# Remaking the instruction order of a planned attention and Fourier-mixing kernel from a table of measured landing times

## The chip, the cores and the metric

The kernel runs on one core of one Trainium2 chip, in a single launch. The metric is the device time in microseconds, the median of several runs. The core has five engines with an instruction stream each: TensorE (PE, matmuls), VectorE (DVE), ScalarE (ACT), GpSimd (POOL) and SyncE (SP, which here only issues transfers). Transfers between device memory and on-chip memory are carried by 16 DMA engines.

## The reference

Batch 4, 8 heads, 768 positions, 64 elements for each head. First comes an attention with a local window of 96 positions and 8 global ones, and a distance bias for each head:

```python
scores = scale * np.matmul(q, k.transpose(0, 1, 3, 2))
is_global = pos[None, :] < 8
is_local = (rel >= 0) & (rel < 96)          # rel = query position - key position
dist = np.where(is_global & ~is_local, 96.0, np.abs(rel))
scores = np.where(is_global | is_local, scores - slopes * dist, -1e9)
a = softmax(scores)
x = heads_side_by_side(a @ v)               # (4, 768, 512)
```

Then a block that mixes with a two-dimensional Fourier transform, normalises, and runs a two-layer MLP:

```python
u = x + np.real(np.fft.fft(np.fft.fft(x, axis=1), axis=2))
un = (u - mean(u)) / np.sqrt(var(u) + 1e-6)
out = u + np.maximum(un @ w_ch1, 0.0) @ w_ch2     # 512 -> 2048 -> 512
```

## The kernel before

The order of all instructions is made by a small planner in Python when the kernel is built. Each piece of work is announced with what it needs, which engine could do it, and how long that takes by a formula. The planner keeps a clock for each engine (`t`) and the time at which each result is there (`tok`); it takes whichever piece could start first, emits its instructions, and moves the clock. Nothing of these clocks is in the program that runs: there the engines wait for each other by semaphores, and each engine takes its instructions in the order in which the planner emitted them.

```python
class Plan:
    SEM = 0.06
    LAND = {("xw", 0, 0): 33.0, ("xw", 0, 1): 37.0, ("xr", 0): 43.0}
    LAT = {"ACT": 0.14, "DVE": 0.12, "POOL": 0.08}
    ...
    def emit(self, place):
        ...
        end = self.t[eng] = ends[i]
        if dma:
            q = "DMA2" if eng == "ACT" or outs and outs[0][0] in ("xw", "xr") else "DMA"
            end = self.t[q] = max(self.t[q], end) + dma
        else:
            lat += self.LAT.get(eng, 0.0)
        for o in outs:
            self.tok[o] = max(end + lat, self.LAND.get(o, 0.0)) if dma else (end + lat, eng)
        ...
    def run(self, streams):
        # [cut] of the heads of the PE streams, and of the work waiting for other
        # engines, take what can start first; emit it; go on until all is done
```

`LAND` holds times before which a transfer's result is not taken as there. `("xw", 0, n)` is the attention output of batch 0 on its way out to device memory, in two parts, and `("xr", 0)` its way back in another row order.

There are four streams of PE work, by order of precedence: `MIX` (Fourier blocks, normalisation), `ATT` (attention), `PH` (first MLP layer) and `PG` (second). The first two may be taken out of order within the next ten pieces.

**Attention, batches 0 and 1.** q, k and v come in for each pair of heads (`hp` 0 to 3; `n` is 4 times the batch plus `hp`). q and k are cast and turned by PE (`trans`, in traces "pt", copied to `qkT`); scores are built in three blocks for a pair ("sc", lines 553, 558 and 563), and ScalarE takes the exp ("ex"). v is cast by GpSimd (line 420, "er"), turned by PE ("pvp") and copied out half by VectorE and half by ScalarE (lines 454 and 455):

```python
def cast_v0(b, hp):
    ...
    pl.later([("POOL", 0.87, cast)], [("ld", n, 2)] + free("er", n), 0.0, [("vc", n)], ...)

def v_place(b, hp):
    ...                                        # 12 matmuls into pvp, then two copies into v16
    ATT.append(([("vc", n), ("c", "id")], BANKS(b), run))
```

`("ld", n, 2)` is the landing of v of pair n. "pgl" and "eg" are the scores of the global positions, "pav" the product with v, lines 709 and 710 its division by the sum, which gives x.

**Loads.** SyncE issues q, k, v; GpSimd issues the weights, eight transfers of 512 KB, which are cast on the way:

```python
pl.later([("SP", 0.55, run)], free(*vat(n)) + [("xi",)] * (n >= HP), 0.0, [("ld", n, 2)], lat=1.7, dma=1.45)
...
pl.later([("POOL", 0.85, lambda i=i: wload(i))], needs, 0.0,
         [("w1" if i < 4 else "w2", i % 4)], lat=2.2, dma=2.75, rank=0, ...)
...
pl.later([("SP", 0.45, hold)], [("w2", 3)], 0.0, [("gate",)])    # batches 2 and 3 load after the last weights
```

**Fourier blocks.** VectorE folds x (lines 754 to 865), PE transforms along the positions ("py", line 891, copied by lines 906 and 908), GpSimd mirrors (lines 926 to 939), PE transforms along the features ("pu", line 971), and VectorE adds x back (lines 990 and 999), which gives u. ScalarE scales the row sum (line 1011), ScalarE or VectorE makes the centred row un (lines 1021 and 1023), and PE turns it ("ptu"), copied to unT (lines 1070 and 1072). ScalarE squares un for the variance (line 1030), and GpSimd turns that into the scale (lines 1037 and 1038).

**MLP.** Rows come in twelve blocks c of 256. For the first layer eight "ph" units of 8 matmuls (128x256) need unT of the block and a quarter of w1; ScalarE or VectorE takes the relu into hT (lines 1096 and 1097). For the second layer "pg" units of 4 matmuls (128x512) need hT and a quarter of w2; VectorE adds u (line 1122), and the rows leave. The last four blocks use a form with fewer multiplications ("pgA", "pgD").

```python
def ph_unit(c, jp):
    needs = [("unT", c), ("w1", jp // 2)] + (free("hT", 5 + c) if jp == 0 else []) + [("CD",)]
    ...
def pg_unit(c, t, part):
    needs = [("h", c, 2 * part), ("h", c, 2 * part + 1), ("w2", part)]
```

PSUM, where PE writes, is divided into two tiles "xx" of two banks each, and two early tiles "C" and "D" of two banks each, which serve batch 0 and parts of batch 1 and are then given up for the accumulators of ph and pg; `("CD",)` is that handover.

Of the kernel before, what the change touches and what calls it, by code (L numbers as in the profile page):

```python
# [17 lines left out]
class Plan:  # L18
# [5 lines left out]


    SEM = 0.06
    LAND = {("xw", 0, 0): 33.0, ("xw", 0, 1): 37.0, ("xr", 0): 43.0}
    LAT = {"ACT": 0.14, "DVE": 0.12, "POOL": 0.08}

    def __init__(self):  # L30
# [56 lines left out]
    def emit(self, place):  # L87
# [11 lines left out]
        for o in outs:  # L99
            self.tok[o] = max(end + lat, self.LAND.get(o, 0.0)) if dma else (end + lat, eng)  # L100
        for u in uses:
# [1373 lines left out]
```

## Time and profile before

| | |
|---|---|
| device time, median of 3 runs | 273.59 us (272.04 to 274.04) |
| profiled span, mean granted PE clock | 272.5 us, 0.987 |
| PE busy | 257.0 us, 94% of the span, 2540 matmuls |
| VectorE busy | 172.0 us, 63% |
| ScalarE busy | 153.4 us, 56% |
| GpSimd busy | 58.3 us, 21% |
| HBM read and written | 31.92 MB and 9.44 MB |

How to read it: the ends of matmuls are modelled, so PE can be "busy" without being at its peak; the distance from one matmul's start to the next says more. A stretch without matmuls is a real hole. In the chain of work that ended last, PE has 73% of the span, DMA 11% and VectorE 8%. Of PE's time ph has 95.4 us and pg 60.2 us. The eight weight transfers take 19.7 us from issue to landing in the median, the three v loads of batch 1 that go to "qs" 16.8 us.

### The profile page before, as it was taken

Reading aid. Unit: us, or ns where it says so; the run is one execution under the profiler, and the core shown is the slowest. Engines: PE = TensorE matmul, PEld = TensorE weight load, DVE = VectorE, ACT = ScalarE, POOL = GpSimd, SP = SyncE. Lnnn points to the kernel's source line nnn. Section 1 sums busy time; section 2 is a strip of 40 time slices with the busy share of each in tenths; the row PEclk is TensorE's granted clock in tenths of the full one; section 3 lists DMA queues with packets and bytes.
Section 4 is the critical chain, followed back from the end, with each engine's and each line's share of the span. In section 5 each row is a group of like instructions: output and inputs, shape, how many; then the busy total and the mean of one; then the engine's idle time right before and its main releaser. Section 6 shows DMA issues by size and latency. Waiting matters only on the chain.

```text
span 272.5 us, 6257 instructions
## 1 busy us (share of the span) xinstructions
PE 257.0 (94%) x2540; PEld 182.6 (67%) x2540; DVE 172.0 (63%) x349; ACT 153.4 (56%) x267; POOL 58.3 (21%) x123
## 2 busy tenths in 40 slices
PE   7898899679999899999999999899999999999994
PEld 3444668347876776667567457576877668888883
DVE  4547855721789665445348976786999765445273
ACT  1579785746639737987683046799435245453310
POOL 1433298133120052311231004021100402010000
PEclk9999999959999999999999999999999999999999
DMA  7999969999569976969776995431036151412022
GB/s 210 290 290 285 330 159 243 214 216 211 140 112 248 260 178 131 182 161 148 176 179 159 188 284 147 75 89 39 2 81 192 38 114 44 98 20 79 0 81 77
DMA packets 75743, 42.03 MB, mean 154 GB/s; under 512 B 32834, under 2 KB 71746, under 8 KB 75714
## 3 DMA queue, kind: packets, MB, share of 16 engines
q1 hardware_dynamic: 68658, 32.71, 51.1%
q0 software_dynamic: 4224, 4.19, 9.3%
q10 hardware_dynamic: 2832, 4.72, 6.8%
q8 instruction: 20, 0.33, 0.5%
q14 instruction: 9, 0.07, 0.1%
HBM read 31.92 MB, written 9.44 MB: 152 GB/s over the span
## 4 chain that ended last, share of the span: by engine, by line
PE 73%; DMA 11%; DVE 8%; SPq 4%; POOL 1%; issue 1%; ACT 1%; DVEq 0%; POOLq 0%; ACTq 0%
PE ph L1090 29%; PE pg L1113 18%; DMA qs<-in_v_dram 6%; PE pgD L1194 5%; PE pgA L1194 4%; PE pav L690 3%; PE sc L563 3%; SPq L371 3%; DMA qs<-in_q_dram 3%; PE pu L971 3%; PE py L891 2%; DMA xd<-x 2%; PE pav L679 1%; PE ptu L1062 1%; SPq L1273 1%
## 5 line engine op out<-in xcount | busy, mean ns | idle before, releaser
L1090 PE MATMUL ph<-unT,w 128*128 128x256 f16 x768 | 95.4, 275 | 0.8 <-DVE hT L1097 0.8
L1090 PEld LDWEIGHTS <-w 128*128 128x128 f16 x768 | 73.1, 99 | 15.6 <-issue 4.8
L1096 ACT ACTIVATE hT<-ph 128x512 f16<-128x512 f32 x75 | 44.6, 596 | 47.5 <-PE ph L1090 47.4
L1113 PE MATMUL pg<-w,hT 128*128 128x512 f16 x256 | 60.2, 379 | 0.0
L1113 PEld LDWEIGHTS <-hT 128*128 128x128 f16 x256 | 24.3, 98 | 24.3 <-issue 0.8
L586 ACT ACTIVATE ex<-sc 128x992 f16<-128x992 f32 (+2 forms) x24 | 21.0, 928 | 8.3 <-PE sc L563 8.3
L583 ACT ACTIVATE er<-sc 128x992 f16<-128x992 f32 (+2 forms) x24 | 21.8, 923 | 3.6 <-PE sc L563 3.5
L598 DVE TENSOR_TENSOR ex<-er,mk 128x992 f16<-128x992 f16 (+2 forms) x24 | 14.8, 626 | 12.0 <-ACT er L583 11.9
L375 ACT ACTIVATE qk<-qs 128x384 f16<-128x384 f32 (+1 forms) x33 | 15.4, 522 | 12.1 <-DMA qkT<-qk 8.3
L939 POOL COPY ww<-zy 128x512 f16<-128x512 f16 x16 | 9.2, 609 | 53.2 <-PE py L891 52.2
L1097 DVE TENSOR_SCALAR hT<-ph 128x512 f16<-128x512 f32 x21 | 14.5, 688 | 8.4 <-PE ph L1090 8.1
L563 PE MATMUL sc<-qkT 64*128 64x256 f16 (+1 forms) x192 | 17.5, 264 | 1.4 <-ACT unT L1070 0.8
L1122 DVE SCALAR_TENSOR_TENSOR u<-pg,sm,u 128x512 f32<-128x512 f32 x16 | 12.0, 747 | 8.8 <-PE pg L1113 8.8
L690 PE MATMUL pav<-v,ex 128*128 128x65 f16 x352 | 16.4, 193 | 0.8 <-DVE x L710 0.7
L563 PEld LDWEIGHTS <-qkT 64*128 64x128 f16 x192 | 5.8, 94 | 16.4 <-issue 14.4
L690 PEld LDWEIGHTS <-ex 128*128 128x128 f16 x352 | 15.3, 97 | 2.1 <-DVE x L710 0.9
L1030 ACT ACTIVATE un<-un 128x512 f16<-128x512 f16 x24 | 14.9, 621 | 1.1 <-DMA unT<-un 1.0
L465 POOL CAST v<-qs 128x768 f16<-128x768 f32 x8 | 7.7, 965 | 35.3 <-DMA qs<-in_v_dram 35.3
L1021 ACT ACTIVATE un<-u,sm 128x512 f16<-128x512 f32 x13 | 9.2, 719 | 10.4 <-DVE sm L994 10.3
L906 ACT ACTIVATE zy<-py 128x1024 f16<-128x1024 f32 (+1 forms) x11 | 9.0, 827 | 10.7 <-PE py L891 10.2
L990 DVE SCALAR_TENSOR_TENSOR u<-pu,xr 128x512 f32<-128x512 f32 x18 | 11.7, 687 | 4.3 <-PE pu L971 4.3
L1194 PEld LDWEIGHTS <-hT 128*128 128x128 f16 x128 | 12.5, 98 | 2.1 <-issue 0.4
(129 smaller groups left out, 373.8 us busy)
## 6 DMA issues: line engine op xcount, KB each, us to landing
out_dram<-u SPq DMA_DIRECT2D x24, 256.0 KB, 2.2
w<-in_moe_w_ch_dram POOLq DMA_DIRECT2D x8, 512.0 KB, 19.7
qs<-in_q_dram SPq DMA_DIRECT2D x9, 384.0 KB, 4.5
qs<-in_k_dram SPq DMA_DIRECT2D x9, 384.0 KB, 5.8
qs<-in_v_dram SPq DMA_DIRECT2D x16, 192.0 KB, 4.2
xr<-xd ACTq DMA_DIRECT2D x3, 768.0 KB, 4.8
u<-in_v_dram SPq DMA_DIRECT2D x5, 384.0 KB, 7.2
w<-in_q_dram SPq DMA_DIRECT2D x4, 384.0 KB, 6.4
```

The source lines that it names most:

```text
L375: A(d, s, AF.Copy)
L563: nc.tensor.matmul(pa[:, s, c0:c0 + cw], TT[n][lo:lo + 64, 1, i * P:(i + 1) * P], TT[n][lo:lo + 64, 0, i * P:i * P + cw], start=(b > 1), s ...
L583: A(mine(), cut(pa), AF.Exp, 0.0, 0.125)
L586: A(cut(expst[hp][:, :, g * 512:g * 512 + (384 if g == 2 else 512)]), cut(pa), AF.Exp, 0.0, 0.125)
L598: VT(o, mine(), m, op=ALU.mult)
L690: nc.tensor.matmul(po[:, jj, hh * 65:(hh + 1) * 65], lhsT, v16[b % 2][:, i, h, 0:65], start=(jp == 0 and a == 0), stop=(a == len(ops) - 1) ...
L1030: A(x, x, AF.Square, accum_out=MV[c][:, a, 2:3])
L1090: nc.tensor.matmul(ph[:, a * CH:(a + 1) * CH], W1[0][:, d, jb * P:(jb + 1) * P], UNT[c][:, d, :], start=(d == 0), stop=(d == ND - 1))
L1096: pl.later([("ACT", act(512), lambda: A(dst, ph, AF.Relu)), ("DVE", dve(512), lambda: V.tensor_scalar_max(dst, ph, 0.0))], [], e, [("h", c ...
L1097: ("DVE", dve(512), lambda: V.tensor_scalar_max(dst, ph, 0.0))],
L1113: nc.tensor.matmul(pg, HT[c][:, jb, t * P:(t + 1) * P], W2[0][:, jb, :], start=(jb == 0), stop=(jb == NJ - 1))
L1194: nc.tensor.matmul(o, lhs(j), rhs(j), start=(first and j == 0), stop=(j == NK - 1), skip_group_check=True)
```

## The change

The table of landing times gets twelve new entries and three changed ones: the round trip of x of batch 0 a little later (changed), and new the four loads of v of batch 1 (pairs n = 4 to 7), and the eight quarters of the weights. It is meant to let the planner order the work by when these results are really there, where it had a formula before. No formula, buffer or piece of work is changed; the instruction order on all engines follows anew from the table.

```diff
     SEM = 0.06
-    LAND = {("xw", 0, 0): 33.0, ("xw", 0, 1): 37.0, ("xr", 0): 43.0}
+    LAND = {("xw", 0, 0): 36.0, ("xw", 0, 1): 37.6, ("xr", 0): 43.3, ("ld", 4, 2): 50.1, ("ld", 5, 2): 55.5, ("ld", 6, 2): 60.9,
+            ("ld", 7, 2): 66.4, ("w1", 0): 45.8, ("w1", 1): 50.6, ("w1", 2): 54.3, ("w1", 3): 57.9, ("w2", 0): 61.6, ("w2", 1): 65.2, ("w2", 2): 68.1, ("w2", 3): 70.7}
     LAT = {"ACT": 0.14, "DVE": 0.12, "POOL": 0.08}
```

The added line moves every line number of the kernel by one: what is L1090 before is L1091 after.

## The prediction

> **What bounds the kernel now.** I read the slices of the page first, then a table by stage, then the chain of waits and the instructions in order of time around the one stage that stands out. The slices say that TensorE (PE) is the bound nearly everywhere, and that there is one hole, in the eighth slice (each is 6.8 us), with a throttled clock in the ninth:
>
> ```profile
> PE   7898899679999899999999999899999999999994
> PEclk9999999959999999999999999999999999999999
> ```
>
> The table by stage (us; then busy time and instructions of PE, its weight loads, VectorE, ScalarE, GpSimd; the clock that PE was granted; DMA) puts figures on it:
>
> ```profile
> 48.00:52.00 4.00, 3.90 (x58) 2.56 (x55) 3.67 (x12) 3.69 (x8) 0.82 (x1) 1.00 1.20 214
> 52.00:56.00 4.00, 0.00 (x0) 0.00 (x1) 0.98 (x2) 1.52 (x6) 0.48 (x1) 0.88 1.20 216
> 56.00:60.00 4.00, 3.60 (x26) 1.76 (x26) 1.64 (x3) 1.71 (x4) 1.27 (x3) 0.50 1.20 216
> 60.00:64.00 4.00, 4.00 (x43) 3.24 (x42) 1.09 (x2) 2.18 (x4) 1.71 (x3) 0.77 1.19 216
> 64.00:68.00 4.00, 4.00 (x47) 2.99 (x45) 0.15 (x1) 3.10 (x6) 0.82 (x1) 1.00 1.24 208
> ```
>
> From 52 to 56 us PE does nothing, while DMA runs at its 216 GB/s, and then PE has half its clock. The chain of waits says what the hole waited for (start, duration, what):
>
> ```profile
> 38.10 0.43 SPq L371
> ...
> 38.63 16.84 DMA qs<-in_v_dram
> 55.47 0.05 issue
> 55.52 0.84 POOL er L420
> 56.36 0.04 issue
> 56.40 0.54 PE pvp L436 x12
> 56.94 1.82 PE ph L1090 x8
> 58.76 0.80 PE sc L553 x2
> 59.55 0.52 PE sc L563 x4
> 60.07 0.96 PE ptu L1062 x8
> 61.03 2.22 PE ph L1090 x16
> ```
>
> A load of v of batch 1 is issued at 38 us and usable at 55.5; GpSimd casts it, and PE turns it ("pvp"). PE takes its instructions as they stand, and the planner had put this pvp before the first matmul of the first MLP layer ("ph"), because the plan had no landing time for v. The ph's own inputs were there: its transposed input unT was written at 51.3 and 53.0, and the weights' first quarter landed early, by the table that the change brings, at 45.8. I take that table as measured on this kernel, for its other entries agree with the trace: the casts of v start at 50.16, 55.52, 61.01 and 66.46, against 50.1, 55.5, 60.9 and 66.4 in the table, and the small transfer that waits for the last weights starts at 70.57, against 70.7.
>
> [...] the gap was 4.43 us, and the clock 0.50 in the next stage. [...] ScalarE's copy of the late v stood idle 4.06 us. So a wrong place in the order blocks whatever stands behind. [...]
>
> **The change, part by part.** No instruction is added that costs anything: both programs have 2540 matmuls, and the order of transfer issues from SyncE and GpSimd up to the last weights is the same in both. Landing times should therefore stay. What moves is the order on each engine. The two programs' PE order is equal up to the third Fourier block of batch 0 ("pu", 48.9 us). Then, before: ptu, pgl, pvp, ptu, pvp (here the hole), ph. After: pgl, ptu, the two score blocks of the last head pair, ptu among them, then ph, ph, ph, ptu, ph, and only then the first pvp; the second comes after eight ph.
>
> *Removed, the hole:* 4.43 us, the idle time that the trace gives for PE ahead of pvp.
>
> *Removed, the slow clock:* the pieces of the chain after the hole against the same pieces at full clock elsewhere in the chain. pvp 0.54 against 0.36 (0.18); 8 ph 1.82 against 0.87 (0.95); the score blocks 0.80 and 0.52, which I halve (0.66); 8 ptu 0.96 against 0.45 (0.51); 16 ph 2.22 against 1.75 (0.47). Sum 2.77 us. Together 7.20 us could come back.
>
> *Added, a new wait at the same place.* I walked the new order from 45 us with the old durations. VectorE now has the copy of qkT (0.96, waiting for PE until 45.9) ahead of the first addition of u, which before ran at 45.18. So the four additions of blocks 0 and 1 end at about 49.9, and the two normalised rows of block 0 are there at about 50.4. ScalarE has, one behind the other: score exp (0.86), small scale, un (0.63), small scale, exp (0.70), small scale, exp (0.90), small scale, eg (0.58), small scale, the copy of unT (1.02), which gives unT at about 52.8, and then two more exps (0.86 and 0.70), done at about 54.6. The two last exps matter, for ph's accumulators take over the PSUM banks "C" and "D", in which the new program has just these two score blocks (the old one had a pvp there, read out by 52.9). PE meanwhile finishes the second score block at about 53.6. So ph starts at about 54.7 and PE idles 1.1 us instead of 4.4, under the length that throttled the clock. After that: ph, ph, a wait for VectorE's relu (0.69), ph, ptu, and ph number 3 at about 57.9; ScalarE's three squares (1.9 us) and a un (0.7) hold back the relu of ph number 1 to about 57.2. I put this second hold at 0.4 us. New waits: 1.5 us.
>
> *Kept, the chain of batch 1.* The last v lands at 66.4 whatever the order. In my walk its averages (pav) end at about 77, within a microsecond of before (VectorE ends the last x at 78.47). VectorE's folds then take about 10 us (78.50 to 88.39 before) and the Fourier block py can't start much before 88. What PE has gained by then it must spend on other work, and the new order has it: between there and the third block of ph it puts 16 more pg matmuls, 16 x 0.216 = 3.5 us, and starts that third batch of ph about 1.5 us earlier than the 105.96 of before. That is a lead of about 5 us at 104. ScalarE has eight exps for the mask table, 0.65 each, ahead of a relu there, so I count 0.8 us lost in this stage.
>
> Later, PE starts follow each other within 0.1 us of what their size needs, apart from gaps of 0.95 us at 90.5, 0.65 at 97.5, 0.96 at 173 and 0.34 at 262 (my reading of the matmuls' starts, width/2400 us each as the 0.216 for 512 columns shows). The new order reshuffles all of that; I let wins and losses cancel. Sum: -7.2 + 1.5 + 0.8 = -4.9; 273.6 - 4.9 = 268.7, and I round to 268.6.
>
> **The rivals.** *The lead is lost again* (time about 272 to 274): if a later stage waits for transfers, PE merely arrives earlier and stands. For it: the loads of batches 2 and 3 are gated by the last weights, 70.6 us, and their transposes go one by one through SyncE. Against it: the transposes of batch 2's first head pair are issued by 95 us and its scores run at 107.9; the third pair's by 122 and its scores at about 131. There are 5 us of slack, as much as the lead.
>
> *The new wait is as long as the old* (about 271 to 273): the walk hangs on ScalarE, which in my walk works without a pause from 46.6 to 54.6. Were it 2 us later still, PE would again idle over 3 us [...]. For it: the planner prices a square at 0.62 where the trace has 0.62 plus a 0.19 read-out. Against it: two squares in a row follow each other at 0.62, so the read-out is mostly hidden.
>
> *More comes back than I count* (about 266.5): the gaps at 90 and 97 go as well, and the 1.1 us wait doesn't appear, as the banks are handed over one by one.
>
> **Range and chances.** The centre is the sum, 268.6. The low end is the whole 7.2 us and the gap at 90: 265.8. The high end is a lead mostly lost: 272.3. A gain over 2% needs 5.5 us, slightly more than my sum, so a little under even; a loss of 2% would need a new hole larger than the old one, and nothing in the order shows one.
>
> **What would show it.** Right: in the slices no clock of 5 in slice nine, PE idle from 52 to 56 under 2 us, ph starting at 54 to 55.5, casts of v by GpSimd for the first pair delayed to about 57 (they stand behind the normalisation scale now) without PE waiting for them, PE equally full after 110. Wrong: a PE hole over 3 us before the first ph with ScalarE or the bank handover named as its end; landings of v or weights shifted by over 2 us; or new holes after 100 us, which would eat the lead.

## The result and the profile after

| | before | after |
|---|---|---|
| device time, median | 273.36 us (272.04 to 274.04, 4 runs) | 269.43 us (268.79 to 269.87, 4 runs) |
| profiled span | 272.5 us | 268.0 us |
| mean granted PE clock | 0.987 | 1.000 |

The ratio is 0.986, with a 95% interval of 0.982 to 0.990; every ratio with an interval here is of fast runs alone. Predicted were 268.6 us and a range of 265.8 to 272.3. The gain is clear of noise and under 2%.

The slices of the page after, the rows of PE and of its clock:

```profile
PE   7899899989999799999999999999999999999994
PEclk9999999999999999999999999999999999999999
```

No slice of the clock is below 9 now, and the 6 that stood in the eighth slice of PE is gone. What is left is a 7 in the fourteenth slice, at 87 to 94 us. The table by stage of the kernel after (the columns are those of the prediction's table):

```profile
52.00:56.00 4.00, 2.94 (x32) 2.28 (x31) 1.46 (x4) 4.00 (x11) 0.26 (x2) 1.00 1.20 216
56.00:60.00 4.00, 4.00 (x50) 3.27 (x49) 1.77 (x4) 2.93 (x8) 3.09 (x5) 1.00 1.20 216
60.00:64.00 4.00, 3.99 (x55) 3.11 (x53) 1.16 (x2) 2.59 (x5) 0.83 (x1) 1.00 1.19 217
...
80.00:88.00 8.00, 6.91 (x44) 4.21 (x43) 7.97 (x16) 5.90 (x12) 0.00 (x0) 1.00 1.09 247
88.00:96.00 8.00, 7.38 (x76) 6.71 (x76) 3.94 (x9) 5.61 (x10) 2.68 (x5) 1.00 0.96 264
```

From 52 to 56 us, where there was no matmul, there are 32, and the clock is full. DMA moves 216 GB/s as before. The hole left there is in the timeline of PE, after (start, duration, what; in brackets the idle time before and what ended it):

```profile
54.30 2.91 PE L1091 MATMUL ph<-unT,w 128*128 128x256 f16 x24 [1.05 <-ACT ex L587]
57.05 0.61 PE L1063 MATMUL ptu<-ident,un 128*128 128x128 f16 x8
57.49 1.04 PE L1091 MATMUL ph<-unT,w 128*128 128x256 f16 x8
58.46 0.36 PE L437 MATMUL pvp<-er,ident 64*64 64x128 f16 x12
```

ph starts at 54.30, after the last two exps on ScalarE, and the first late pvp stands behind four ph. The casts of v start at 56.62 (the first, late, but nothing waits for it), 58.80, 61.41 and 66.85; their loads land at 50.43, 55.86, 61.29 and 66.73, 0.4 us later than before (50.04, 55.47, 60.89, 66.33). So nothing came sooner: PE waits for less.

From one matmul's start to the next the median is 56, 109 and 216 ns for 128, 256 and 512 columns on 128 rows, in both traces; that fits 2400 columns a microsecond and 2.5 ns besides (55.8, 109.2 and 215.8). So, to count what came back, I take for each matmul its "start gap": the start of the next one, less its own start, less its width at 2400 columns a microsecond. In the sums those 2.5 ns are taken off each, and a negative gap, of matmuls that overlap, counts as none. A matmul at half clock shows as a gap too: before, eight ph took 1.82 us at a clock of 0.50, against 0.87 at full clock. The sums by stage, from the two traces:

| us | 0 to 48 | 48 to 64 | 64 to 80 | 80 to 96 | 96 to 112 | 112 to 216 | whole |
|---|---|---|---|---|---|---|---|
| before | 11.59 | 8.22 | 0.84 | 0.96 | 1.18 | 5.78 | 29.24 |
| after | 11.79 | 3.10 | 0.54 | 1.90 | 0.74 | 6.09 | 24.84 |
| difference | +0.20 | -5.12 | -0.30 | +0.94 | -0.44 | +0.31 | -4.40 |

The whole, -4.40, is the difference of the spans, 4.5. The only stage that got worse by more than a few tenths is 80 to 96. There the timeline of ScalarE, after, shows how work taken in a fixed order stands on a load:

```profile
79.94 3.85 ACT L1309 ACTIVATE mk<-dist 128x640 f16<-128x640 f16 x6
85.50 0.35 ACTq L738 DMA_DIRECT2D xr<-xd  x1
85.90 0.94 ACT L376 ACTIVATE qk<-qs 128x384 f16<-128x384 f32 x2 [2.10 <-DMA qs<-in_q_dram]
86.74 1.35 ACT L1309 ACTIVATE mk<-dist 128x640 f16<-128x640 f16 x2
88.00 0.58 ACT L1097 ACTIVATE hT<-ph 128x512 f16<-128x512 f32 x1
```

and PE, after, behind it:

```profile
88.62 1.03 PE L1091 MATMUL ph<-unT,w 128*128 128x256 f16 x8 [1.72 <-ACT hT L1097]
```

Six mask exps, then the issue of x's way back, then a cast of q of batch 2, for which ScalarE stood idle 2.10 us, then two more mask exps, and only then the relu for which PE waited: a start gap of 1.88 us. The chain that ended last, after, says where that load was held up (start, duration, what):

```profile
42.86 28.09 DMA w<-in_moe_w_ch_dram
...
73.16 5.21 DMA qs<-in_v_dram
...
79.35 6.13 DMA qs<-in_q_dram
```

The last weights land at 70.95, and they gate the loads of batch 2; a load of v lands at 78.37, GpSimd casts it, and only then does the load of q start, which lands at 85.48. So PE, which now comes earlier, meets transfers that do not: the prediction's first rival, in small. Two old gaps, 0.95 and 0.65 at 90 and 97, are gone in return.

### The profile page after: what moved, and what is told of

It is laid out like the page before. It is cut to its first block, busy times and chain, and to the rows that moved or that the text cites. A ratio compares the mean times of both kernels' runs of the same rounds, so it can differ in the third digit from the quotient of the medians.

```text
span 268.0 us, 6248 instructions
## 1 busy us (share of the span) xinstructions
PE 255.5 (95%) x2540; PEld 181.3 (68%) x2540; DVE 172.0 (64%) x349; ACT 151.1 (56%) x263; POOL 60.4 (23%) x127
## 3 DMA queue, kind: packets, MB, share of 16 engines
q0 software_dynamic: 4224, 4.19, 9.5%
## 4 chain that ended last, share of the span: by engine, by line
PE 64%; DMA 20%; ACT 5%; SPq 4%; DVE 2%; POOL 2%; issue 1%; ACTq 0%; POOLq 0%
PE ph L1091 26%; PE pg L1114 12%; DMA w<-in_moe_w_ch_dram 10%; PE pgD L1195 5%; DMA qs<-in_q_dram 5%; PE py L892 4%; PE pgA L1195 4%; PE sc L564 3%; PE pu L972 3%; DMA u<-in_v_dram 3%; PE pav L691 3%; ACT ex L587 2%; DMA qs<-in_v_dram 2%; SPq L372 2%; SPq L506 2%; ACT qk L376 2%
## 5 line engine op out<-in xcount | busy, mean ns | idle before, releaser
L1091 PE MATMUL ph<-unT,w 128*128 128x256 f16 x768 | 94.1, 273 | 2.8 <-ACT hT L1097 1.7
L1091 PEld LDWEIGHTS <-w 128*128 128x128 f16 x768 | 72.7, 98 | 17.2 <-issue 6.2
L1097 ACT ACTIVATE hT<-ph 128x512 f16<-128x512 f32 x78 | 46.2, 596 | 41.7 <-PE ph L1091 41.6
L376 ACT ACTIVATE qk<-qs 128x384 f16<-128x384 f32 (+1 forms) x29 | 13.8, 527 | 14.1 <-DMA qs<-in_q_dram 5.6
L1098 DVE TENSOR_SCALAR hT<-ph 128x512 f16<-128x512 f32 x18 | 12.4, 691 | 11.6 <-PE ph L1091 11.6
L466 POOL CAST v<-qs 128x768 f16<-128x768 f32 x8 | 6.6, 827 | 51.5 <-DMA qs<-in_v_dram 51.5
L1038 POOL TENSOR_SCALAR sm<-sm 128x2 f32<-128x2 f32 x12 | 2.3, 194 | 57.9 <-ACT un L1031 57.8
L907 ACT ACTIVATE zy<-py 128x1024 f16<-128x1024 f32 (+1 forms) x12 | 10.0, 846 | 9.2 <-PE py L892 8.1
L940 POOL COPY ww<-zy 128x512 f16<-128x512 f16 x16 | 9.9, 651 | 22.9 <-PE py L892 20.8
```

What stands on the lines that cost most here:

```text
L376: A(d, s, AF.Copy)
L1091: nc.tensor.matmul(ph[:, a * CH:(a + 1) * CH], W1[0][:, d, jb * P:(jb + 1) * P], UNT[c][:, d, :], start=(d == 0), stop=(d == ND - 1))
L1097: pl.later([("ACT", act(512), lambda: A(dst, ph, AF.Relu)), ("DVE", dve(512), lambda: V.tensor_scalar_max(dst, ph, 0.0))], [], e, [("h", c ...
L1098: ("DVE", dve(512), lambda: V.tensor_scalar_max(dst, ph, 0.0))],
```

## The experiments

Of the 120 runs of the kernel before beside the experiments (267.95 to 277.62 us) 24 kept a granted clock of 0.997 or more, with a median of 270.1 us, and the other 96 have one of 273.8; how often each comes is part of what the order does, so medians over all runs are compared here.

**Which entries do it?** Three kernels bring in one group of entries each, with everything else as before. Beside them, and beside the fourth, before had 273.61 us.

```diff
 e1_v_only:  + ("ld", 4, 2): 50.1, ("ld", 5, 2): 55.5, ("ld", 6, 2): 60.9, ("ld", 7, 2): 66.4
 e2_w_only:  + the eight quarters of the weights
 e3_x_only:  ("xw", 0, 0): 36.0, ("xw", 0, 1): 37.6, ("xr", 0): 43.3
```

> Only the four landings of v of batch 1 are put into the old table. In the built order the pvp of the second pair already stands behind ph number 3. Theory (the gain is the hole ahead of the first ph and the slow clock behind it, and any order that has the late pvp behind ph brings it): no PE hole over 2 us between 48 and 64 us, granted clock 1.0 there, time 269 to 270.5 us. Rival (the landings of the weights are what the gain hangs on): the stage from 56 to 72 us gets waits of PE for weights of 1.5 us or more, and the time is above 271.5.

> Only the eight landings of the weights are put into the old table. The built PE order is that of the kernel before up to about the third batch of ph. Theory: the hole of 4.4 us and the half clock are still there, time 272 to 274. Rival (weights' landings are what counts): below 271.

> Only the three times of the round trip of x of batch 0 are changed. The loads of v of batch 1 are announced behind that round trip, so the planner moves them too, and in the built order the pvp stands behind ph as in the changed kernel. Theory: the hole is gone here as well, clock 1.0; but the first pg (weights' fifth quarter, landing near 61.6) stands behind the sixth ph, so PE waits there up to 1.5 us; time 269 to 271.5. Rival (v's own entries are needed): a PE hole over 3 us again at some pvp between 50 and 68 us, time above 272.

*v alone* had 271.76 us (269.36 to 273.02). The hole before ph is gone (a gap of 0.65 us is left, ahead of a score block), but one of 4.75 us has opened at 86: the time is that of the rival, through another wait than the rival named. PE, v alone, its timeline:

```profile
91.10 1.22 PE L1090 MATMUL ph<-unT,w 128*128 128x256 f16 x5 [4.59 <-ACT hT L1096]
```

On ScalarE there, in v alone, the mask exps, casts of q or k and the issue of x's way back stand ahead of the relu:

```profile
84.93 0.94 ACT L375 ACTIVATE qk<-qs 128x384 f16<-128x384 f32 x2 [2.58 <-DMA qs<-in_q_dram]
87.98 0.35 ACTq L737 DMA_DIRECT2D xr<-xd  x1
88.38 1.36 ACT L1308 ACTIVATE mk<-dist 128x640 f16<-128x640 f16 x2 [2.51 <-DMA qs<-in_v_dram]
...
90.47 1.06 ACT L1096 ACTIVATE hT<-ph 128x512 f16<-128x512 f32 x2
```

After it the clock was 0.57 from 88 to 96 us. The hole had moved 30 us on.

*The weights alone* had 272.19 us (266.99 to 275.36). Up to the third batch of ph PE has the old order. In the run with the profile the second v was cast at 52.05, where before shows 55.52, and PE waited for it only this long (weights alone, PE):

```profile
52.92 0.36 PE L436 MATMUL pvp<-er,ident 64*64 64x128 f16 x12 [1.22 <-POOL er L420]
```

Its span was 267.7 us, less than the changed kernel's: in the old order the time hangs on when v lands, here some 3.5 us sooner than in the trace of before. It is not the usual run: 15 of the 20 had a clock of 0.994 or less, as most runs of before have, so there the hole stands, as expected, if the clock is taken as its sign.

*x alone* had 271.69 us (271.17 to 274.1). Against what the prediction held, this alone puts the late pvp behind four ph, with the same 1.05 us ahead of the first ph as in the changed kernel. It then meets weights that the plan took as there: 1.31 us of idle PE at 61, ended by w2's first quarter, a start gap of 1.14 at 73 and one of 2.73 at 88.

Building the table in parts says more. With v's four entries left out, and x and the weights kept, the planner makes the same program as the changed kernel's, instruction for instruction on all five engines. It still does with only the first x entry (33.0 to 36.0) and the weights. So of the fifteen entries six do nothing, and of the three for x the first by itself gives the order of *x alone*.

**What was the slow clock worth?** The old order with the hole filled: 76 matmuls of 128 columns, which feed nothing, ahead of the pvp that waits.

```diff
+            if n == 5:
+                idle(76)
```

> The kernel before, with 76 matmuls of 128 columns that compute nothing used, put ahead of the late pvp: they fill the hole and do not shorten it. Theory (the slow clock is a consequence of the idle time and costs 2.8 us by itself): granted clock 1.0 from 52 to 64 us, the late pvp still at about 56.4 us, time 2.3 to 3.2 us below the kernel before. Rival (the slow clock slows only work that then waits for something else anyway): time within 0.8 us of the kernel before.

It had 273.42 us (271.67 to 275.45) against 273.61, and a ratio of 1.003 (1.000 to 1.006). PE, the hole filled:

```profile
51.59 4.41 PE L429 MATMUL pvp<-eg 128*128 128x128 f16 x76
55.93 0.36 PE L438 MATMUL pvp<-er,ident 64*64 64x128 f16 x12
...
60.67 0.36 PE L438 MATMUL pvp<-er,ident 64*64 64x128 f16 x12 [0.39 <-POOL er L420]
...
66.10 0.36 PE L438 MATMUL pvp<-er,ident 64*64 64x128 f16 x12 [0.76 <-POOL er L420]
...
97.23 0.96 PE L973 MATMUL pu<-t,ww 128*128 128x128 f16 x14 [1.20 <-POOL ww L941]
```

The clock is full throughout, and yet little comes of it. The faster PE now waits for the third and fourth v (0.39 and 0.76). Its pvp of the last v starts 1.68 us earlier than before (66.10 against 67.78), but in this run that v was cast 1.24 us earlier, too (65.22 against 66.46): 0.44 is left for the clock. The trace of before says the same:

```profile
66.46 0.82 POOL L420 CAST er<-u 128x768 f16<-128x768 f32 x1 [3.57 <-DMA u<-in_v_dram]
67.78 0.36 PE L436 MATMUL pvp<-er,ident 64*64 64x128 f16 x12
```

Its cast of the last v ends at 67.28 and its pvp starts at 67.78, so a PE at full speed could have been there 0.5 us sooner and no more. Then a wait for batch 1's Fourier block at 97 takes more (third batch of ph at 105.00 against 105.96). In the old order most of the 2.77 us of slow clock lay beside landings that PE had to wait for anyway. The median alone doesn't show this, for the filler takes its 4.41 us whenever v lands: in this run the second v was cast by 55.10, and the filler held its pvp back by another 0.8 us, which the later waits for v swallowed. Where v lands sooner still the filler must cost time, so gain and loss are mixed in 273.42, and what the clock alone is worth over many runs stays open.

**The wait that was added.** In the changed kernel the two last score blocks of batch 1 are kept off the banks that ph takes over.

```diff
-        ATT.append((..., BANKS(b), run))
+        ATT.append((..., ("xx",) if n == 7 and g else BANKS(b), run))
```

> The changed kernel itself, beside more runs of the kernel before. Theory (the old order puts a late, luck-dependent load of v ahead of work that is ready; the new order has it behind): median 269 to 270.5 us, granted clock 0.998 or more in nearly every run and a spread of at most 3 us, against 268 to 278 us and clocks of 0.98 to 1.00 for the kernel before. Rival (the new order is as open to luck, and the first runs were lucky): a spread as wide as that of the kernel before, and clocks under 0.995 in a third of the runs or more.

> The changed kernel, with the last two score blocks of batch 1 kept out of the PSUM tiles C and D, which become ph's accumulators. Theory (the 1.05 us hole ahead of the first ph waits for ScalarE to read out C and D): the hole falls below 0.4 us and ph starts by 53.6 us; time 0.3 to 1.2 us below the changed kernel. Rival (ph is held by its input unT or by the weights): ph still starts at 54 us or later.

The changed kernel had 269.38 us again (268.42 to 270.68, 20 runs, all with a clock of 0.997 or more; before 273.61 beside these four; ratio 0.991, 0.987 to 0.994). In this second trace of it the second v landed at 51.76 and the span is 267.2, against 55.86 and 268.0 in the first; the old order had 267.7 us with that landing at 51.99 (the weights alone) and 272.5 with it at 55.47 (before). So the new order hardly minds when v lands, as the theory has it.

With the banks it had 268.78 (265.52 to 273.85, 20 runs). The gap of 1.21 directly ahead of ph is gone and ph starts at 53.60, but two of 0.44 and 0.55 stand a little earlier, both ended by ScalarE. PE, with the banks:

```profile
51.09 0.61 PE L1063 MATMUL ptu<-ident,un 128*128 128x128 f16 x8 [0.28 <-ACT eg L656]
52.09 0.56 PE L554 MATMUL sc<-dist,sid 128*128 128x480 f16 x2 [0.39 <-ACT unT L1071]
...
111.97 0.50 PE L564 MATMUL sc<-qkT 64*128 64x256 f16 x4 [2.54 <-DVE u L991]
```

So the banks decide which work waits, and ScalarE, busy 7.71 of the 8 us from 48 to 56, for how long: the gaps from 48 to 64 us add up to 2.65 instead of 3.02 in the changed kernel's run beside it. The gap at 86 is gone as well. But PE meets a new one at 109 to 112 (start gap 2.70), and the clock falls to 0.66 after it. VectorE, with the banks, shows what it stood on:

```profile
110.61 0.69 DVE L991 SCALAR_TENSOR_TENSOR u<-pu,xr 128x512 f32<-128x512 f32 x1 [4.68 <-DMA out_dram<-u]
```

The third Fourier addition needs a buffer of u. The store that frees it was issued at 105.75, after SyncE had spent 98.5 to 104.2 on four transposes and then two loads of v, and it landed at 110.53. The widest spread of all the changed versions is that of this one, and it has two parts: eleven of the 20 runs kept a clock of 0.999 or more and have a median of 266.55 us, the nine others, of which this trace is one, had 0.994 or less and 269.51 to 273.85. So where the clock stays full, the time is nearly 3 us under the changed kernel's.

**The hole at 86.** The mask exps need only to wait for the end of the Fourier transform along the positions ("mask later"); and then the plan is told, too, that the two loads of batch 2's second pair land at 88.

```diff
 e7, e8:  -  [("c", "dist"), ("x", 1, 3, 2)], 0.0, [("mk", hp)]
          +  [("c", "dist"), ("y", 1, 0, 3)], 0.0, [("mk", hp)]
 e8:      +  ("ld", 9, 0): 88.0, ("ld", 9, 1): 88.0
```

> The changed kernel, with the eight mask exps on ScalarE made to wait for batch 1's Fourier blocks, so that they leave the place ahead of the relus of the third batch of ph. The cast of q of the second pair of batch 2 (its load lands near 85.5 us) is still ahead of those relus in the built order. If the mask exps make the PE hole at 86.6 us (1.88 us): it falls below 0.7 us and the time is 1 us below the changed kernel. If it is mostly the cast's load: a hole of 1 to 1.8 us remains and the time is within 0.6 us of the changed kernel.

> As the kernel before this one, and the planner is told that the two loads land at 88 us, so that their casts stand behind the three relus. Theory (ScalarE's first-in first-out queue, with a load's cast ahead of ready relus, makes the hole at 86.6 us): hole below 0.7 us, time 0.8 to 1.8 us below the changed kernel. Rival (PE would wait there for the Fourier block's folds on VectorE in any case): the hole moves to the first py at 88 to 89 us and the time is within 0.5 us of the changed kernel.

They had 267.82 us (267.43 to 268.96) and 267.76 (267.53 to 268.13). With the mask later the gap is still 1.31, because the cast of q still stands there. With the cast moved too it is gone (no start gap over 0.12 there), but PE in that kernel stands further on:

```profile
95.43 0.73 PE L972 MATMUL pu<-t,ww 128*128 128x128 f16 x10 [1.25 <-POOL ww L940]
```

The chain of batch 1, with GpSimd's mirror copy at its end, takes what the second edit gave. The sums of the start gaps are 22.79 and 22.57 (after: 24.84). For the first of them only some 0.6 of the 2.05 is from the hole at 86; 1.3 comes from 112 to 216, where the order also changed.

**All together, and one entry less.**

```diff
 e9:   e6 + e7          e10:  e6 + e8          e12:  e10 + ("ld", 11, 0): 111.7
 e11:  the changed kernel with ("xw", 0, 0): 33.0, ("xw", 0, 1): 37.0, ("xr", 0): 43.0
```

> The changed kernel with both of the edits tried before: the two last score blocks of batch 1 kept off the accumulators' banks, and the mask exps put behind the last Fourier transform along the positions. Theory A (each hole is worth its own length, and they add): start gaps before the first ph of at most 0.7 each, no gap over 1.4 at 84 to 90, and none over 1 at 105 to 112; time 265 to 266.5. Theory B (a hole that is taken away comes back further down): the wait of 2.7 at 109 of the kernel with the banks alone stays, since the store of u that frees the buffer stands at the same place in SyncE's queue, behind transposes; time 267.5 to 269.

> As the run before it, and with the two loads for the second head pair of batch 2 taken as landing at 88 in the plan. Here the store of u of the second row block stands two places earlier in SyncE's queue, ahead of the next loads of q and k. Theory A: all three holes under 1 us, time 264.5 to 266. Theory B: the third Fourier addition of batch 1 still waits for a store of u at 105 to 111, gap over 1.5, time 267 to 269.

> The changed kernel with the three entries for the round trip of x put back to 33.0, 37.0 and 43.0; the four loads of v and the eight weights stay in the table. The first late pvp then stands ahead of the first ph again, the second behind four ph. Theory A (what matters is that the v landing at 55.5 stands behind ph, whatever entry brings that about): the hole ahead of the second pvp is gone, the first ph waits for a v that landed at 50 and so less than 1.5 us, median within 1 us of the changed kernel's 269.4. Theory B (the x entries do more than that, for they also order the Fourier blocks of batch 0): median 271 to 273, with a hole of over 1.5 us at another place before 100 us.

> The kernel of the run with banks, mask and cast, and one more measured landing in the plan: the load of q of the last head pair of batch 2 at 111.7, where its trace has ScalarE standing 2.26 on it ahead of a relu. On ScalarE the cast now stands behind that relu. Theory A (a late load at the head of a first-in queue is the whole of that hole): the gap of 2.03 at 111 shrinks to under 0.6, the sum of the start gaps falls from 22.7 to about 21, median 265.5 to 266.5. Theory B (the hole comes back as another wait within the next 20 us, on a store of u, a transpose or the next load): gaps of over 1.2 at 105 to 130, median 267 to 268.5.

*Banks and mask* had 268.14 us (266.77 to 269.5), *banks, mask and cast* 267.44 (267.15 to 267.83), beside 273.74 for before. The first shows no wait at 109 in its trace (the rival missed that): its store of u was issued at 102.62 and landed at 106.2, against 105.75 and 110.53 with the banks alone. Its gap at 85 is 1.45, and its sum of gaps is the lowest of all, 21.49, with a span of 265.0; its other runs are slower, and its median is the rival's. In the second the hole came back at 111, in the shape known from 86: ScalarE stood 2.26 us on a load of q, ahead of a relu, and PE 1.86: the rival's time, but by a load and not by the store that it named. With that load in the plan as well (e12) it was 268.63 us (266.78 to 270.9; before 272.92), no better, as its rival said; the run with its trace was the longest of the six, so which waits came in its place isn't shown.

*Without the x entries* it was 272.77 us (271.59 to 275.04). The hole ahead of pvp is gone, a gap of 0.65 is left before ph, and the time comes close to before's all the same. PE, without the x entries:

```profile
108.56 1.03 PE L1090 MATMUL ph<-unT,w 128*128 128x256 f16 x8 [1.70 <-ACT hT L1096]
...
169.17 0.62 PE L1062 MATMUL ptu<-ident,un 128*128 128x128 f16 x8 [1.10 <-DVE u L990]
```

On ScalarE four casts and three squares stand ahead of the relu at 108, and VectorE's additions of u hold PE at 168 to 171 (start gaps of 1.27, 1.00 and 0.57). So this rival was right on the time and wrong on the place: I had put the new hole before 100 us. It is a lead lost again, as in the prediction's first rival, but to the order of computing and not to transfers. This trace is of the fastest of the four runs; the others had clocks of 0.985 to 0.991, as the traces with 2.5 us and more of idle PE at one place have (0.985 to 0.993), so they probably stood longer somewhere, which no trace shows.

## Why the prediction was right, and where its steps were not

*The hole is removed:* right. PE waits for no v between 52 and 63 us. The "Wrong" signs that it named didn't come: landings moved by 0.4 us, and no gap over 3 us stands before ph.

*The reason given for the hole, that "the plan had no landing time for v":* wrong as the cause of this change's effect. v's entries can do the work (v alone), but so does x's one entry (x alone), and in the changed kernel v's four are without effect. The reading behind it is from the diff, of the planner's loads: `[("xi",)] * (n >= HP)` ties the later loads of v to the return of x in the plan, and so a later x makes a later v. That tie I take from the code; what the runs show is that x's entry alone moves the pvp.

*The slow clock, 2.77 us:* a term that doesn't stand by itself. With the old order and a full clock some 0.4 us of it was left at the last pvp, and no gain shows in the time. It is also a little large: from the late pvp to the end of the 16 ph PE needs 6.78 us before and 4.19 with the clock kept full, 2.59 less. The 0.36 for pvp comes from another view than its 0.54 (the chain has 0.29 at full clock), and the score blocks take 0.50 and 0.31 at full clock, not half of 0.80 and 0.52. In the new order the late pvp stand further back as well, so that PE at full clock has other work while they land. What the prediction had right was the sum for 48 to 64 us: it had -7.2 + 1.5 = -5.7 there, and the start gaps show -5.1. How long PE stood and what clock went with it, by the traces: 4.43 us, then 0.50 from 56 to 60 (before); 4.59 us, and 0.57 from 88 to 96 (v alone); 2.54 us, then 0.66 from 112 to 116 (with the banks); 2.57 of the 8 us from 88 to 96, and 0.79 over them (x alone). 1.05 and 1.72 us left it at 1.00 (after, 52 to 56 and 88 to 96). From which length on the clock falls isn't shown.

*The new wait, 1.1 + 0.4 us:* right in place and nearly in size: start gaps of 1.22 and 0.13, and 0.37 for an average of x at 63.8. ph starts at 54.30 (predicted 54.7), ph number 3 at 57.49 (57.9), the first pair's v is cast at 56.62 (57). That the banks cause it is only half right: kept off them, PE waits for ScalarE at two other places, for 0.99 in all. It was ScalarE's queue, on which the walk hung.

*The lead of 5 us at 104:* right. The third batch of ph starts at 104.36, 1.60 us earlier than before, with 16 more pg done by then, 3.45 us: 5.05.

*0.8 us lost on ScalarE before a relu:* right in kind, too small and not whole. The gap is 1.88 us, for the walk had the mask exps but not the cast of q, which waited for a load. The two old gaps that left take most of it back: 80 to 112 us lost 0.50.

*"Wins and losses cancel" later:* +0.31 from 112 to 216 us, nearly so here. Without the x entries it fails, so this was luck of this order and no rule.

The sum -4.9 stands against -4.4 in the gaps and -3.9 in the medians. The rival that had more come back, by the gaps at 90 and 97, was right that they go, and wrong that nothing takes their place. The rival that had the lead lost to transfers was right in kind for the 1.88 us at 86, which end a chain from the last weights, and wrong in size: most of the lead stayed.

## What to carry to other kernels

Where engines take their work in a fixed order (ScalarE here stood 2.10 us on a load, ahead of a relu for which PE waited), put into the plan when a transfer is really there, and look for the whole chain that hangs on it: one entry for x alone did as much here as four for v (271.69 and 271.76 us), which did nothing once it was there. A hole removed counts only once the next waits have been walked: a wait on a load or a store, in a queue taken in order, took back gains 30 to 60 us further on (PE stood 4.59 us in v alone, 2.54 with the banks, 1.86 with banks, mask and cast). Before counting a slow clock as lost time, look how long ahead of its use the next transfer lands: here the last v was cast 0.50 us before its pvp, so of 2.77 us no more than that could come back there.

## What was not expected of the hardware

The same transfer lands at quite different times. The weights alone have the old order up to there, and their second v is cast at 52.05 us, where before has 55.52; the cast of the last v starts at 62.98 with the weights alone, 65.22 with the clock kept full and 66.46 before. The time of before moves by over 9 us over its runs; the changed kernel's is steadier, 268.42 to 270.68. The 14 traces hint at what sets the landing: the first load of v of batch 1 lands at 45.1 to 45.4 us in the four where it was issued 0.44 to 0.50 us after the first load of weights, and at 49.1 to 50.4 in the ten where it was 0.53 to 1.15 us. Whether this is the cause wasn't tried.

The old order with its hole filled by matmuls that feed nothing was no faster (ratio 1.003, 1.000 to 1.006), though the trace shows the clock at 1.00 instead of 0.50.
